# A plain second matrix product for the first 256-token unit, and its weight combinations spread out, in a fused attention and feed-forward kernel

## The chip, the core and the metric

The kernel runs on one core of one Trainium2 chip. The metric is the device time of one execution in microseconds (us); the profile is one more execution, recorded by the hardware profiler. The engines are TensorE (PE, with its weight loads as PEld), VectorE (DVE), ScalarE (ACT), GpSimd (POOL) and SyncE (SP, which issues nearly all the DMAs). Each engine works through its own instructions strictly in the order in which they were written, and they wait for each other by semaphores.

## What is computed

Attention in which each query keeps its 32 highest scores, for 8 batches of 8 heads with 576 tokens and 64 numbers per head, and then a two-layer feed-forward block on 4608 tokens:

```python
scores = q @ k.T / 8                   # per head, 576 x 576
kth    = the 32nd largest of each row
attn   = softmax(where(scores >= kth, scores, -1e9))
x      = (attn @ v), heads side by side # 4608 x 512
h      = x @ w_in                       # 512 -> 2048
g      = h - tanh(h)
out    = g @ w_out                      # 2048 -> 512
```

All in float32 on the chip.

## The kernel before, in words

**Steps.** The attention is cut into 144 steps; `plan` (L987) lists them. A step is one tile of 128 queries for a pair of heads. Batch 0 is steps 0 to 17, batch 1 is steps 18 to 35. The main loop (L1169) runs iteration n and works on several steps at once:

- `scores(n+1)` (L339): TensorE makes the scores of the next step in PSUM (L351), ScalarE copies them to SBUF (L359).
- `search(n)` (L362): VectorE finds the 32nd largest by folding (L381 to L389) and by rounds of MAX8 and MATCH_REPLACE8 (L393 to L404). It starts with L381, so the starts of L381 are the starts of the steps.
- `threshold(n)` (L409): GpSimd turns the result into a threshold, `tb` (L418), `nb` (L427).
- `mask(n-1)` (L430): ScalarE (L437) and GpSimd (L440, the tile `z`) strike out what is below the threshold; GpSimd notes a check in `bad` (L444).
- `expo(n-1)` (L456): ScalarE takes the exponentials (L460), GpSimd adds a small number to the sums in `rd` (L470).
- `invert(n-2)` (VectorE, L479, early in the search of iteration n), `divide(n-2)` (ScalarE, L486), `turn_z` (VectorE transposes the tile, L518, at the end of the search). `spread_keys` sends it through DRAM (L531, L534), and `values` (L568) multiplies by v on TensorE (L582). Batch 0 goes another way: TensorE transposes the tile.

**Units.** Tokens whose heads are all done form a unit: 256 tokens, except that the first 256 tokens of batch 0 are two units of 128. The feed-forward of a unit is a list of items (`ffn`, L965), appended to `work`, and `deal` (L1161) puts items between the attention's instructions, about three to a step. `rate` (L1143) sets how many: it spreads what is in `work` evenly until the next unit comes, using each unit's `items` (30 for 256 tokens).

**First matrix.** Items 0 to 15 of a 256-token unit (`ffn_full`, L956, which calls `ffn_h`, L630) are the product with `w_in`. `by_columns` (L623) splits each matmul into two halves of 64 output rows. After each odd item ScalarE takes tanh (L652) and a copy (L653), and GpSimd subtracts (L654, a 128x512 tensor).

**Second matrix.** For a 128-token unit it is plain: `ffn_o` (L656) adds 16 matmuls of 128x512 into one PSUM bank, ScalarE copies the bank (L671), SP sends it out (L673). For a 256-token unit it is Strassen-Winograd: seven products (`ORDER`, L830) of half-sized blocks in place of eight, as 14 items (`ffn_p`, L865; `product`, L836) of matmuls with 256 columns. The left factors need four sums of parts of g (`sum_up`, L817, GpSimd, L828: 8 tensors of 128x512 a unit, some issued as halves), the results need joins (L877, GpSimd).

**Weight combinations.** The right factors need T1 to T4, made once from `w_out` by `combine` (L690) on GpSimd: 16 subtractions of 128x512 (`COMBINE`, L709). `w_out` is four tensors of blocks b11, b12, b21, b22. T3 = b12 - b22 goes to the tensor `more`. T1 = b12 - b11 is written over b12 (L698), after which the plain second matrix can't be used any more. T2 = b22 - T1 (L700) and T4 = b21 - T2 (L705) follow; two halves of T2 and two of T4 are also stored in DRAM (`outgoing`, `send_kept`, L934; L702, L707), because `more` has room for only one of the two at a time: `bring` (L831, DMA L834) loads them back in items 4 and 11 of every unit's second matrix. `combine_next` (L939) does one combination per call, T3 from iteration 17 on, T2 and T4 from iteration 20 on; it is called by the second 128-token unit's `ffn_small_o` (L950) and by **every** item of `ffn_full`. In the profile the four T3 and the first T1 fall into the last items of the 128-token unit (214 to 226 us), and the other three T1, the four T2 and the four T4 into the first twelve items of the first 256-token unit (231 to 268 us).

Of the kernel before, what the change touches and what calls it, by code (L numbers as in the profile page):

```python
# [9 lines left out]
ALU = mybir.AluOpType  # L10
# [15 lines left out]
class Step:  # L26
# [4 lines left out]
    def __init__(self, b, hp, qt, unit, col, i=0, nq=1, pe=False, part=0):  # L31
        self.b, self.hp, self.qt, self.unit, self.col = b, hp, qt, unit, col
        self.part = 0 if pe else part
        self.i, self.nq, self.pe = i, nq, pe
        self.rem = qt == J
        self.last = i == nq - 1

        self.lag = 2 if pe else LAG


class Unit:
# [3 lines left out]
    def __init__(self, blocks, tag):  # L45
        self.blocks, self.tag = blocks, tag
        self.n = 128 * len(blocks)
        self.combines = False
        self.tail = False
        self.items = 16 if self.n == 128 else 30  # L50
        self.xT = None
        self.g = []
# [3 lines left out]
def kernel(  # L56
# [9 lines left out]
    nc = tc.nc  # L66
    P = nc.NUM_PARTITIONS
# [9 lines left out]
    CD = DM // P  # L77
    CF = DFF // P
# [4 lines left out]
    WJ = 4  # L83
# [32 lines left out]
    def next_h(name):  # L116
        bank[0] ^= 1
        return h_bank(bank[0], name)
# [19 lines left out]
    whole = {  # L138
        "T3": [more[:, 1024 * i : 1024 * (i + 1)] for i in range(2)],
        "T4": [more[:, 2048:3072], more[:, 3072:4096]],  # L140
        "T2": [more[:, 3072:4096], et_pe[:, 0:1024]],
    }
    whole = {x: [y.rearrange("p (m n) -> p m n", n=2 * P) for y in ys] for x, ys in whole.items()}
# [73 lines left out]
    def half(t):  # L217
        return slice(t * D, (t + 1) * D)
# [349 lines left out]
    def values(n):  # L568
# [41 lines left out]
        if n in done:  # L610
            work.extend(ffn(u))
# [44 lines left out]
    def ffn_o(u, i, part):  # L656
        if part == 0:
            cur[u] = next_h("ops")
        for f in range(2 * part, 2 * part + 2):
            o = f * u.n + i * P  # L660
            nc.tensor.matmul(
                cur[u][:],
                u.g[0][:, o // 512, o % 512 : o % 512 + P],
                w_out[f // FJ][:, f % FJ, :],
                start=(f == 0),
                stop=(f == CF - 1),
            )
        if part < CF // 2 - 1:
            return
        ot = thpool.tile([P, DM], FP32, tag="th", name="ot")  # L670
        nc.scalar.copy(ot[:], cur[u][:])  # L671
        for rows, dst in u.blocks[i]:
            nc.sync.dma_start(dst, ot[rows, :])  # L673
# [3 lines left out]
    def corners(x):  # L677
        x = x.rearrange("p (m r) n -> p m r n", r=2)
        return [[x[:, :, r, c * 2 * P : (c + 1) * 2 * P] for c in range(2)] for r in range(2)]
# [10 lines left out]
    def combine(x, j):  # L690

        (b11, b12), (b21, b22) = corners(w_out[j][:])
        k, ms = j // 2, slice(2 * (j % 2), 2 * (j % 2) + 2)
        t2 = whole["T2"][k][:, ms, :]
        if x == "T3":
            nc.gpsimd.tensor_tensor(whole["T3"][k][:, ms, :], b12, b22, ALU.subtract)
        elif x == "T1":
            nc.gpsimd.tensor_tensor(b12, b12, b11, ALU.subtract)  # L698
        elif x == "T2":
            nc.gpsimd.tensor_tensor(t2, b22, b12, ALU.subtract)  # L700
            if k == 0:
                outgoing.append((called[0], lambda: nc.sync.dma_start(kept["T2"][:, ms, :], t2)))  # L702
        else:
            t4 = temps[j % 2] if k else whole["T4"][k][:, ms, :]
            nc.gpsimd.tensor_tensor(t4, b21, t2, ALU.subtract)  # L705
            if k:
                outgoing.append((called[0], lambda: nc.sync.dma_start(kept["T4"][:, ms, :], t4)))  # L707

    COMBINE = [("T3", j) for j in range(WJ)] + [("T1", j) for j in range(WJ)]  # L709
    COMBINE += [(x, j) for j in (2, 3, 0, 1) for x in ("T2", "T4")]  # L710

    def quarters(u, k):

# [103 lines left out]
    def sum_up(u, k, x, ms=slice(0, 4)):  # L817

        (a11, a12), (a21, a22) = quarters(u, k)
        s1 = sums[k]  # L820
        out_, a, b, op = {
            "S1": (s1, a21, a22, ALU.add),
            "S3": (a21, a21, a11, ALU.subtract),
            "S2": (a11, s1, a11, ALU.subtract),
            "S4": (a12, a12, a11, ALU.subtract),
        }[x]
        engine = nc.vector if u.tail else nc.gpsimd
        engine.tensor_tensor(out_[:, ms], a[:, ms], b[:, ms], op)  # L828
# [102 lines left out]
    combined, now = [0], [0]  # L931
    called, outgoing = [0], []

    def send_kept(age):  # L934

        while outgoing and outgoing[0][0] <= called[0] - age:
            outgoing.pop(0)[1]()

    def combine_next():  # L939

        called[0] += 1
        send_kept(4)
        if combined[0] < len(COMBINE):
            x, j = COMBINE[combined[0]]
            if now[0] < (17 if x == "T3" else 20 if x in ("T2", "T4") else 0):
                return
            combine(x, j)
            combined[0] += 1

    def ffn_small_o(u, part):  # L950

        ffn_o(u, 0, part)
        if u.combines:
            combine_next()

    def ffn_full(u, item):  # L956

        ffn_h(u, item)
        combine_next()
        if item in (8, 9):  # L960
            sum_up(u, 0, ("S1", "S3")[item - 8])
        if item in (12, 13):
            sum_up(u, 1, ("S1", "S3")[item - 12], slice(0, 2))

    def ffn(u):  # L965

        nh = CF * u.n // (2 * P)
        full = len(u.blocks) == 2
        if u.tail:
            nh = 0  # L970
            for item in range(2 * len(ORDER)):
                yield CD * WJ, u, lambda item=item: ffn_s(u, item)
        for item in range(nh):
            f = (item + 1) * CF // nh - 1
            yield CD * (f // FJ + 1), u, lambda item=item: (ffn_full if full else ffn_h)(u, item)
        if not full:
            for part in range(CF // 2):
                yield CD * (WJ + part // 2 + 1), None, lambda part=part: ffn_small_o(u, part)
            return
        for item in range(2 * len(ORDER)):  # L980
            yield 2 * WJ * CD, None, lambda item=item: ffn_p(u, item)
# [5 lines left out]
    def plan():  # L987
        steps.clear(), done.clear()

        def block(b, qt):  # L990
            return [(slice(0, P), out[b * S + qt * P : b * S + (qt + 1) * P, :])]

        rest = None
        for b in range(B):
            if b % 4 == 0:
                rest = Unit(
                    [
                        [(half(i), out[(b + k + i) * S + JP : (b + k + i + 1) * S, :]) for i in range(2)]
                        for k in (0, 2)
                    ],  # L1000
                    "xTr",
                )

            parts = [(0, 1), (2, 3)]
            if b == 0:
                parts[0:1] = [(0,), (1,)]
            for a, qts in enumerate(parts):
                unit = Unit([block(b, qt) for qt in qts], "xT")
                unit.tail = b == B - 1 and a == len(parts) - 1
                if unit.tail:  # L1010
                    rest.tail = True
                    unit.items = rest.items = 4 * len(ORDER)
                pe = b == 0
                unit.combines = pe and a == 1
                for hp in range(NHP):
                    for i, qt in enumerate(qts):
                        steps.append(Step(b, hp, qt, unit, 0, i, len(qts), pe, a))
                    if hp == NHP - 1:
                        done[len(steps) - 1] = unit
                    if hp % 2 and a == (0 if b == B - 1 else len(parts) - 1):  # L1020
                        steps.append(Step(b, hp - 1, J, rest, b % 4 * R, pe=pe, part=a))
                        if hp == NHP - 1 and b % 4 == 3:
                            done[len(steps) - 1] = rest
        for g, after in zip(steps, steps[1:]):
            if after.pe and not after.rem and not g.pe:
                g.lag = 3
# [3 lines left out]

    def run(exact):
        plan()
        turned_pe[0] = not exact
        combined[0] = 0
# [237 lines left out]
```

## Time and profile before

| what | us |
|---|---|
| median of 3 timed runs (lowest, highest) | 1476.77 (1475.81, 1477.08) |
| time of the profiled execution | 1476.01 |
| its span, first to last instruction | 1474.2 |
| PE busy | 1365.6 (93%) |
| DVE busy | 1321.5 (90%) |
| POOL busy | 1090.2 (74%) |
| ACT busy | 1033.2 (70%) |
| start of step 20, 25, 50 (L381) | 227.88, 278.47, 490.81 |
| one 128x512 subtraction on POOL (L654) | 1.28 |
| one 128x576 subtraction on POOL (L440) | 1.44 |

How to read it: each row of a group names line, engine, operation, output and inputs; the busy time is the sum over the group. A timeline row gives start and duration, and in brackets how long the engine had stood idle and which instruction let it go on. A row of a windows table gives, for one stretch of time, how long each engine was busy in it; with the starts of L381 as borders each row is one step of the attention.

### The profile page before, as it was taken

How to read it: one execution, taken by the hardware profiler on the slowest of the kernel's cores; microseconds unless marked ns; L12 is line 12 of the kernel's file. 1: busy time of each engine (PE TensorE's matmuls, PEld its weight loads, DVE VectorE, ACT ScalarE, POOL GpSimd, SP SyncE). 2: the span in 40 equal slices, each digit the busy share in tenths (PEclk: the TensorE clock that was granted, in tenths of full speed). 3: DMA queues.
4: the chain of work that ended last, by engine and by line, in shares of the span. 5: the costliest groups of instructions: out<-in, count | busy, mean ns of one | idle time of the engine just before them, and what ended most of it. 6: DMA issues, size and time to landing. Idle time of an engine off the chain costs nothing.

```text
span 1474.2 us, 37773 instructions
## 1 busy us (share of the span) xinstructions
PE 1365.6 (93%) x13316; PEld 871.1 (59%) x13316; DVE 1321.5 (90%) x4968; ACT 1033.2 (70%) x1921; POOL 1090.2 (74%) x1581
## 2 busy tenths in 40 slices
PE   4667899889999898999999999999999999999998
PEld 2455565455565555656556666666565666656885
DVE  7999988899999999999999999999999999886411
ACT  4776677778787777777687777777777777664421
POOL 3777679968788686969696969696969697868211
PEclk9787999999999999999999999999999999999999
DMA  9955103676767676686767767777676667643320
GB/s 273 381 184 168 53 21 90 169 195 167 196 173 197 164 183 180 160 209 152 190 152 192 179 174 177 194 168 185 167 184 172 171 167 200 157 141 108 89 53 32
DMA packets 241255, 241.90 MB, mean 164 GB/s; under 512 B 177440, under 2 KB 186144, under 8 KB 233888
## 3 DMA queue, kind: packets, MB, share of 16 engines
q1 hardware_dynamic: 238688, 239.09, 60.7%
q8 instruction: 108, 1.77, 0.5%
q14 instruction: 91, 0.75, 0.2%
q10 hardware_dynamic: 2368, 0.30, 0.2%
HBM read 153.47 MB, written 85.85 MB: 162 GB/s over the span
## 4 chain that ended last, share of the span: by engine, by line
PE 46%; DVE 36%; POOL 9%; DMA 3%; ACT 3%; issue 2%; SPq 0%; DVEq 0%; ACTq 0%; POOLq 0%
PE hps L626 14%; PE hx L626 10%; PE hy L626 8%; DVE m L401 7%; PE av L582 5%; PE scps L351 5%; DVE top L393 5%; DVE rest L404 5%; DVE zx L518 5%; DVE ab L387 3%; POOL z L440 3%; DVE top L404 2%; DVE ab L382 2%; POOL g L654 2%; DVE scps L381 2%
## 5 line engine op out<-in xcount | busy, mean ns | idle before, releaser
L440 POOL TENSOR_TENSOR z<-sc,z 128x576 f32<-128x576 f32 x288 | 406.8, 1435 | 66.4 <-ACT z L437 66.0
L626 PE MATMUL hps<-xT,w_in 128*64 128x256 f32 x3584 | 412.2, 385 | 3.7 <-ACT g L653 3.7
L626 PEld LDWEIGHTS hps<-xT,w_in 128*64 128x64 f32 x3584 | 252.5, 138 | 157.1 <-issue 30.6
L486 ACT ACTIVATE z<-z,rd 128x576 f32<-128x576 f32 x252 | 181.2, 767 | 88.3 <-DVE rd L479 87.9
L460 ACT ACTIVATE z<-z,nb 128x576 f32<-128x576 f32 x288 | 221.9, 776 | 13.1 <-POOL z L440 13.0
L437 ACT ACTIVATE z<-sc,tb 128x576 f32<-128x576 f32 x288 | 208.3, 776 | 24.6 <-POOL tb L418 19.8
L654 POOL TENSOR_TENSOR g<-g,th 128x512 f32<-128x512 f32 x128 | 163.9, 1281 | 63.4 <-ACT g L653 61.9
L393 DVE MAX8 top<-ab 128x8 f32<-128x144 f32 x864 | 194.7, 296 | 0.0
L359 ACT COPY sc<-scps 128x1152 f32<-128x1152 f32 x144 | 161.0, 1118 | 44.7 <-PE scps L351 43.9
L351 PE MATMUL scps<-kT,qT 64*64 64x288 f32 x2016 | 154.6, 422 | 30.3 <-DVE top L389 27.1
L518 DVE STREAM_TRANSPOSE zx<-z 128x1152 f32<-128x1152 f32 x126 | 171.7, 1363 | 7.6 <-ACT z L486 5.1
L401 DVE MAX8 m<-rest 128x8 f32<-128x168 f32 x576 | 161.8, 323 | 0.0
L401 DVE MAX8 m<-top 128x8 f32<-128x144 f32 (+1 forms) x576 | 153.1, 308 | 0.0
L626 PE MATMUL hx<-w_out,g 128*64 128x256 f32 x1088 | 129.2, 385 | 2.5 <-POOL g L654 2.4
L626 PE MATMUL hy<-more,g 128*64 128x256 f32 x1088 | 125.4, 380 | 0.0
L351 PEld LDWEIGHTS scps<-kT,qT 64*64 64x64 f32 x2016 | 66.7, 133 | 97.6 <-issue 26.4
L418 POOL TENSOR_SCALAR tb<-m 128x1 f32<-128x1 f32 x288 | 85.9, 307 | 35.0 <-DVE m L401 34.6
L387 DVE TENSOR_TENSOR ab<-scps,sc 128x576 f32<-128x576 f32 x144 | 107.7, 748 | 0.0
L626 PEld LDWEIGHTS hx<-w_out,g 128*64 128x64 f32 x1088 | 76.2, 138 | 49.9 <-POOL g L654 5.7
L626 PEld LDWEIGHTS hy<-more,g 128*64 128x64 f32 x1088 | 76.7, 137 | 43.7 <-issue 6.7
L652 ACT ACTIVATE th<-hps 128x512 f32<-128x512 f32 x128 | 75.1, 587 | 38.7 <-PE hps L626 35.3
L444 POOL TENSOR_SCALAR bad<-top,tb 128x3 uint8<-128x3 f32 x288 | 96.6, 343 | 0.1
(215 smaller groups left out, 2464.7 us busy)
## 6 DMA issues: line engine op xcount, KB each, us to landing
there<-zx SPq DMA_DIRECT2D x56, 1152.0 KB, 4.8
spare<-there SPq DMA_DIRECT2D x224, 288.0 KB, 5.5
more<-kept_T SPq DMA_DIRECT2D x33, 512.0 KB, 4.2
there<-zx SPq DMA_DIRECT2D x14, 576.0 KB, 7.2
spare<-there SPq DMA_DIRECT2D x56, 144.0 KB, 3.2
out_dram<-ot SPq DMA_DIRECT2D x31, 256.0 KB, 3.0
vb<-in_v_dram SPq DMA_DIRECT2D x48, 128.0 KB, 5.0
kin<-in_k_dram SPq DMA_DIRECT2D x82, 72.0 KB, 4.4
```

Of the source, the lines that this page charges most:

```text
L351: nc.tensor.matmul(ps[i * R : i * R + w, t, s, 0:S2], qT[g.b, hp, g.part][half(t), o : o + w], kT[g.b, hp][half(t), ks], start=True, stop= ...
L359: nc.scalar.copy(sc[:], ps[:, :, :, 0:S2])
L387: nc.vector.tensor_tensor(low[:, :, :, 0:W2], thirds(near), thirds(far), ALU.min)
L393: nc.vector.max(top[:, t, o : o + 8], low[:, t, i, :])
L401: nc.vector.max(m[:, t, m8], seen[i][t])
L437: nc.scalar.activation(zv[:, t, :], scf[:, t, :], AF.Relu, bias=tb[:, t : t + 1], scale=-BIG)
L440: nc.gpsimd.tensor_tensor(zv[:, t, :], scf[:, t, :], zv[:, t, :], ALU.subtract)
L460: nc.scalar.activation(x["zv"][:, t, :], x["zv"][:, t, :], AF.Exp, bias=x["nb"][:, t : t + 1], scale=scale, accum_out=den[:, t : t + 1],)
L486: nc.scalar.activation(x, x, AF.Copy, scale=rds[n][:, g.i, t : t + 1])
L518: nc.vector.transpose(tiles(zx, g.nq)[:, :, :, g.i, :].rearrange("p c k j -> p k c j"), z[:].rearrange("p (k c j) -> p k c j", c=NG, j=G),)
L626: nc.tensor.matmul(acc[half(t)], lhs[:, half(t)], rhs, start=start, stop=stop, skip_group_check=True)
L654: nc.gpsimd.tensor_tensor(g, g, th[:], ALU.subtract)
```

## The change

The unit of the tokens 256 to 511 of batch 0, the first of 256 tokens, is marked `plain`. Its second matrix is no longer `ffn_p` but 16 items of `ffn_plain_o`: for each of its two blocks of 128 tokens eight calls of `ffn_o`, each with two of the 16 k-blocks, now through `by_columns` with 512 columns. Its `items` are 32 in place of 30. T1 is made last of all, and only in the items of the next unit, since it overwrites b12. T2 is computed as b11 - T3, which equals the old b22 - T1. `combine_next` is called on odd items only, in `ffn_full` and in `ffn_plain_o`, and `send_kept` waits two calls in place of four. The four sums of g, the joins and the two `bring` transfers of this one unit are not issued. All later units are as before.

In the order of the built instructions VectorE's list is identical before and after. On the other engines the lists differ from step 19 to about step 35, by single places in a few steps of the unit after that, and nowhere later.

```diff
+        self.plain = False
...
-            nc.tensor.matmul(
+            (by_columns if u.plain else nc.tensor.matmul)(
                 cur[u][:],
-                u.g[0][:, o // 512, o % 512 : o % 512 + P],
+                u.g[o // 2048][:, o % 2048 // 512, o % 512 : o % 512 + P],
                 w_out[f // FJ][:, f % FJ, :],
...
-            nc.gpsimd.tensor_tensor(t2, b22, b12, ALU.subtract)
+            nc.gpsimd.tensor_tensor(t2, b11, whole["T3"][k][:, ms, :], ALU.subtract)
...
-    COMBINE = [("T3", j) for j in range(WJ)] + [("T1", j) for j in range(WJ)]
-    COMBINE += [(x, j) for j in (2, 3, 0, 1) for x in ("T2", "T4")]
+    COMBINE = [("T3", j) for j in range(WJ)]
+    COMBINE += [(x, j) for j in (2, 3, 0, 1) for x in ("T2", "T4")] + [("T1", j) for j in range(WJ)]
...
-    def combine_next():
+    def combine_next(plain=True):
         called[0] += 1
-        send_kept(4)
+        send_kept(2)
         if combined[0] < len(COMBINE):
             x, j = COMBINE[combined[0]]
-            if now[0] < (17 if x == "T3" else 20 if x in ("T2", "T4") else 0):
+            if plain and x == "T1" or now[0] < (17 if x == "T3" else 20 if x in ("T2", "T4") else 0):
                 return
...
+    def ffn_plain_o(u, item):
+        ffn_o(u, item // (CF // 2), item % (CF // 2))
+        if item % 2:
+            combine_next()
+
     def ffn_full(u, item):
         ffn_h(u, item)
-        combine_next()
+        if item % 2:
+            combine_next(u.plain)
+        if u.plain:
+            return
...
+        if u.plain:
+            for item in range(CF):
+                yield 2 * WJ * CD, None, lambda item=item: ffn_plain_o(u, item)
+            return
...
+                unit.plain = pe and a == len(parts) - 1
+                if unit.plain:
+                    unit.items = 32
```

## The prediction, as put on record

> **What bounds the kernel now.** I took the starts of L381 first: in batch 1 a step takes 8.44 to 8.57 us as long as nothing holds VectorE up, and from step 25 to step 50 nearly all do. Just ahead of that, where the edited code runs, steps are longer. The table of windows with one row per step (20 to 25) shows it; its columns after the length are PE, PEld, DVE, ACT and POOL busy, the granted clock, the DMA share and GB/s.
>
> ```profile
> core 0: us, PE busy (x) PEld busy (x) DVE busy (x) ACT busy (x) POOL busy (x), PEclk, DMA share, GB/s
> 227.88:237.58 9.70, 9.70 (x123) 6.50 (x121) 8.51 (x33) 8.58 (x17) 9.54 (x15) 1.00 0.15 33
> 237.58:248.66 11.08, 10.33 (x94) 5.52 (x88) 8.66 (x34) 7.62 (x15) 10.91 (x16) 1.00 0.06 14
> 248.66:257.10 8.44, 5.97 (x44) 3.10 (x46) 8.40 (x34) 5.66 (x11) 8.28 (x11) 0.80 0.93 259
> 257.10:267.58 10.48, 9.71 (x96) 5.99 (x94) 8.60 (x35) 7.67 (x14) 10.32 (x13) 1.00 0.59 139
> 267.58:278.47 10.89, 8.50 (x66) 4.40 (x62) 8.72 (x36) 7.87 (x15) 10.72 (x16) 0.84 0.95 255
> 278.47:286.91 8.44, 6.13 (x64) 3.86 (x64) 8.40 (x35) 7.19 (x15) 8.19 (x16) 1.00 0.19 38
> ```
>
> In steps 21, 23 and 24 VectorE works only 8.6 to 8.7 us of 10.5 to 11.1, while POOL is busy nearly throughout; step 20 is another case, there PE is busy for all 9.70 us. The waits of VectorE from 237 to 279 us, and then those of POOL from 214 to 302 us:
>
> ```profile
> DVE rd L479 <- POOL rd L470: 4.8, 3, 2.4
> DVE top L389 <- POOL bad L444: 1.5, 1, 1.5
> DVE scps L381 <- ACT sc L359: 1.2, 1, 1.2
> ```
>
> ```profile
> POOL z L440 <- ACT z L437: 0.4, 1, 0.4
> ```
>
> So VectorE waits for POOL, and POOL for hardly anything: 85.7 us busy of those 88. Its timeline in step 23, and VectorE's wait that follows from it:
>
> ```profile
> 258.99 1.28 POOL L705 TENSOR_TENSOR more<-w_out,more 128x512 f32<-128x512 f32 x1
> 260.22 1.27 POOL L828 TENSOR_TENSOR et<-g 128x512 f32<-128x512 f32 x1
> 261.47 0.59 POOL L418 TENSOR_SCALAR tb<-m 128x1 f32<-128x1 f32 x2
> ...
> 262.36 0.23 POOL L470 TENSOR_SCALAR rd<-den 128x2 f32<-128x2 f32 x1
> 262.67 1.28 POOL L654 TENSOR_TENSOR g<-g,th 128x512 f32<-128x512 f32 x1
> ```
>
> ```profile
> 262.62 0.17 DVE L479 RECIPROCAL rd<-rd 128x2 f32<-128x2 f32 x1 [1.83 <-POOL rd L470]
> ```
>
> A combination (L705) and a sum of g (L828) stand ahead of the threshold and `rd` that VectorE needs.
>
> **What the Trainium skill says.** "GPSIMD Engine Reference", section 3.1, puts a two-input elementwise operation at about 2.6 cycles an element and 4497 ns for 2048 float32; a quarter, 1.1 us, is my estimate for 512. The trace has 1.24 to 1.28 us a tensor start to start, and I use 1.25. "TensorEngine Tiling (Array Packing)", section Key Properties, says that tiles work in parallel. The trace agrees at 256 columns: an item of halves (16 records) takes as long as the same work at full width (two k-blocks of 128x512, 4 records), 1.76 to 1.8 us:
>
> ```profile
> 199.97 3.60 PE L661 MATMUL ops<-w_out,g 128*128 128x512 f32 x8
> ```
>
> ```profile
> 256.14 3.67 PE L626 MATMUL hps<-xT,w_in 128*64 128x256 f32 x32
> ```
>
> No run here shows halves with 512 columns. "TensorE: Matmul & The Clock Gate", section What's actually happening, says an idle window halves the array's clock. The trace agrees in part: after 2.62 us without work scores took 1.62 us in place of 1.20 (at 251.12) and the windows above show 0.80 and 0.84; after 3.45 us (at 314.81) they took 1.20 all the same.
>
> **The change part by part.** A batch-1 step costs POOL 2.78 (L440 twice) + 0.60 (bad) + 1.17 (tb, nb, rd) = 4.55 us. In 8.5 us that leaves room for (8.5 - 4.55)/1.25 = 3.2 tensors of 512.
>
> *Combinations and sums around steps 20 to 24.* I counted the other POOL tensors between the `z` pairs of consecutive steps, z(18) to z(24), by the order of the built instructions. Before: 3 (and two small xTr), 4, 5, 6, 1.6, 2.6 (a half counts 0.6); the z pairs of the trace are 9.10, 9.52, 10.73, 12.03, 6.49 and 7.76 us apart, and 4.55 + 1.25 x 6 = 12.05 confirms the price. After: 1 (and xTr), 4, 2, 2, 4, 2, and then 1. So the three intervals of 9.5 to 12.0 us become 9.55, 7.05 and 7.05, and the overload is gone.
>
> *Does the step then reach VectorE's own time?* `rd` is needed 3.45 us after the start of a step (237.58 to 241.03, where L479 began to wait), and the threshold ahead of it may begin 7.1 us after the start of the step before, 1.34 us ahead. With 1.17 us for tb, nb and rd, POOL may be 1.34 + 3.45 - 1.17 = 3.6 us late. I walked the new order through steps 21 to 25 with durations of the trace. The threshold begins at 238.9, 247.3, 256.9, 264.2, 273.7; `rd` is ready 1.0, 1.1, -0.1, 1.1 and 0.1 us ahead of its need. So some 0.1 us of waiting stays, and two steps have no reserve. ScalarE's copy of the next scores is ready 0.8, 0.5, 0.6 and 1.2 us early.
>
> *Gain.* Steps 21 to 24 took 11.08 + 8.44 + 10.48 + 10.89 = 40.89 us, and VectorE was busy for 8.66 + 8.40 + 8.60 + 8.72 = 34.38. The difference is 6.5 us. Less 0.1 for the wait and 0.2 for the thin reserves: **-6.2 us**. The 1.2 us of step 20 stay, being PE's (no idle from 218.9 on), and PE's list is the same up to there.
>
> *PE.* The unit's second matrix goes from 14 items at 1.76 = 24.6 to 16 at 1.76 = 28.2: +3.5 us. Hidden: a step with three items is 3 x 1.76 + 1.13 (scores) + 1.1 (half of a `values` of 2.16) + 0.4 (transposes) = 7.9 us of 8.5, and in steps 25 to 30, where the plain items lie, PE waits today for VectorE's L389 (2.31, 1.33 and 3.45 us). Without that cover it costs the 3.5. The order has three items in each step from 21 to 29, and the next unit begins no later against the steps. For a 512-column item I take the full-width price, 1.76; the lower end is the same, since the same columns stream; the upper, if the halves took turns, is 3.5.
>
> *T1, moved into the next unit.* Around steps 30 to 35 POOL's counts become 4, 2, 5, 3.2, 3.2, 3.6, over the room at times; walked through in the same way, it is up to 2.5 us late, within the 3.6 that cost nothing: 0. T1 waits for the plain items' reads of w_out, which PE finished a step earlier; queued behind it are the threshold and `rd` of that step, and behind those VectorE. If the reserve is gone, each tensor costs VectorE up to 1.25.
>
> *ScalarE.* Seven copies of 0.36 us become two of 0.59: -1.3 us, off the path.
>
> *DMAs and SP's queue.* Two loads of 512 KB are not issued (7.4 us to landing, beside other transfers), two stores of 256 KB out go earlier. On SP the stores of kept T2 wait for their POOL subtraction at 264.2 and 273.7; ahead of them stand the transfer of the transposed tile and the loads, which end near 267 and 272, and behind the second stands a tile transfer that waits for L518 to about 280. So nothing waits: 0. The first `values` of batch 1 needs its tile at 259.8, and I have it landed at about 258.5: 1.3 us of reserve.
>
> *Sum.* Later instruction lists are nearly the same and VectorE's is identical, so the 6.2 us go through to the end. The profiled execution was 1476.01 us (its span of 1474.2 and 1.8 around it), 0.76 below the median; both move alike: 1476.01 - 6.2 = 1469.8, against the median 1476.77 - 6.2 = 1470.6.
>
> **The rivals.** *Halves take turns at 512 columns.* A 512-float output fills its PSUM bank, and only 256 columns have been seen to overlap. A step has room for (8.5 - 1.13 - 1.1 - 0.3)/3 = 2.0 us an item, so the loss is 16 x (item - 2.0) against a gain of 6.2: slower than before from 2.4 us an item, and at 3.5 it is 24 - 6 = +18, 1495 us. Against it: the 256-column rows. *The queue moves.* T1 beside sums and g's in steps 30 to 33 exceeds the reserve, or the two tight steps miss it; some 3 us come back: 1473.6. For it, reserves of 0 to 1.1 us; against it, only isolated tensors are left. *PE takes over.* With POOL gone PE fills 7.9 of 8.5 us; a late tile or a clock of 0.8 in two steps costs 2 x 1.2: 1473. *The change doesn't do what it says*, because the shift is taken up by PE's waits after step 50 (steps of 8.8 to 10 us there): 1476.8. Against it, those follow the same lists. *More*: step 20's 1.2 and some later waits go too: 1468.
>
> **How the numbers follow.** Forecast 0.62, more 0.07, queue moves or PE takes over 0.14, no effect 0.11, halves in turn 0.06. "Faster by over 0.2%" means over 2.95 us, about what a measurement tells from no change: 0.62 + 0.07 + 0.11 of the 0.14 = 0.80. Within: 0.03 + 0.11 = 0.14. Slower: 0.06. The range reaches from 1467.0 (a gain of 9.8, all of step 20 and 2.4 later) to 1474.2 (the partial cases with 0.6 for the median's own spread); it leaves out no effect and halves in turn.
>
> **What would show it.** Right: L381 of step 25 at about 272 in place of 278.47, step 50 at about 484.6, VectorE's waits for POOL in steps 21 to 24 under 0.5 us, no `sum_up` before step 32, plain items of 8 records in 1.76 us. Wrong: L479 waiting for `rd` in steps 22, 24 or 30 to 35, plain items over 2 us, or the lead of step 50 lost before the end.

## The result and the profile after

| | kernel before | changed kernel |
|---|---|---|
| median of the first timed runs, us | 1475.7 (6 runs, 1473.45 to 1477.08) | 1468.05 (6 runs, 1466.62 to 1470.23) |
| ratio to before, 95% interval | | 0.9951, 0.9938 to 0.9964 |
| time of the profiled execution, its span | 1476.01, 1474.2 | 1468.51, 1466.6 |
| POOL busy, PE busy | 1090.2, 1365.6 | 1078.7, 1366.4 |
| start of step 20, 25, 50 | 227.88, 278.47, 490.81 | 226.03, 270.08, 482.39 |
| steps 20 to 24 together | 50.59 | 44.05 |
| steps 25 to 30 together | 50.88 | 50.87 |

The changed kernel is faster by 7.65 us, and the place is the one that the prediction named: five steps lost 6.54 us, the six after them nothing. From here on line numbers of the changed kernel are one higher than those of before in this region (L381 is L382, L470 is L471, L479 is L480). "Steps 20 to 24" always means the time from the start of step 20 to the start of step 25.

The table of windows of the changed kernel, one row for each of the steps 20 to 25, with the columns that the table of before has:

```profile
226.03:235.74 9.71, 9.71 (x123) 6.51 (x121) 8.52 (x34) 8.59 (x17) 9.46 (x16) 1.00 0.15 33
235.74:244.33 8.59, 8.59 (x82) 4.90 (x78) 8.56 (x34) 7.04 (x13) 6.87 (x10) 1.00 0.08 18
244.33:252.77 8.44, 8.44 (x83) 4.96 (x80) 8.40 (x35) 7.94 (x17) 8.14 (x13) 1.00 0.90 260
252.77:261.51 8.74, 8.06 (x82) 5.01 (x80) 8.50 (x34) 6.88 (x15) 8.56 (x13) 1.00 0.63 136
261.51:270.08 8.57, 8.52 (x64) 3.62 (x62) 8.54 (x36) 7.91 (x16) 8.41 (x12) 1.00 0.92 263
270.08:278.52 8.44, 6.83 (x54) 2.90 (x52) 8.40 (x35) 6.14 (x13) 8.26 (x14) 1.00 0.63 132
```

In steps 21 to 24 (rows two to five) the length is now VectorE's own busy time to within 0.24 us. POOL dropped from 10.91 to 6.87 us in step 21. Step 20 is as long as before, with PE busy throughout. The granted clock is 1.00 in every row, where it had 0.80 and 0.84 in two steps.

The waits of VectorE from 235 to 271 us, of the changed kernel (in all, times, longest):

```profile
DVE scps L382 <- ACT sc L360: 1.2, 1, 1.2
DVE rd L480 <- POOL rd L471: 0.2, 1, 0.2
```

The 4.8 us for `rd` are 0.2, and the 1.5 for `bad` are gone. The 1.2 for ScalarE's copy of the scores belong to step 20. POOL's timeline in step 23, and VectorE's `rd` there:

```profile
252.92 1.28 POOL L655 TENSOR_TENSOR g<-g,th 128x512 f32<-128x512 f32 x1
254.16 1.27 POOL L706 TENSOR_TENSOR spare<-w_out,et 128x512 f32<-128x512 f32 x1
255.42 0.58 POOL L419 TENSOR_SCALAR tb<-m 128x1 f32<-128x1 f32 x2
255.96 0.25 POOL L428 TENSOR_SCALAR nb<-m 128x2 f32<-128x2 f32 x1
256.30 0.23 POOL L471 TENSOR_SCALAR rd<-den 128x2 f32<-128x2 f32 x1
```

```profile
256.56 0.17 DVE L480 RECIPROCAL rd<-rd 128x2 f32<-128x2 f32 x1 [0.20 <-POOL rd L471]
```

Two tensors stand ahead of the threshold, as before: now the subtraction for g (L655) and a combination, then a combination and a sum of g. What has changed is when POOL comes to them: 0.15 us after the start of the step (252.92 against 252.77) in place of 1.89 us (258.99 against 257.10). Between the two `z` pairs ahead of them it has two tensors to make where it had five. The wait is 0.20 in place of 1.83 us. It is the step that the walk had given a reserve of -0.1 us.

### The profile page after: what moved, and what is told of

It reads as the page before. It is cut to its first block, busy times and chain, and to the rows that moved or that the text cites. A ratio compares the mean times of both kernels' runs of the same rounds, so it can differ in the third digit from the quotient of the medians.

```text
span 1466.6 us, 37560 instructions
## 1 busy us (share of the span) xinstructions
PE 1366.4 (93%) x13220; PEld 864.3 (59%) x13220; DVE 1321.3 (90%) x4968; ACT 1032.7 (70%) x1916; POOL 1078.7 (74%) x1568
## 4 chain that ended last, share of the span: by engine, by line
PE 43%; DVE 37%; POOL 7%; DMA 5%; ACT 4%; issue 2%; SPq 1%; ACTq 0%; DVEq 0%; POOLq 0%
PE hps L627 13%; PE hx L627 10%; PE hy L627 8%; DVE m L402 7%; PE av L583 5%; PE scps L352 5%; DVE top L394 5%; DVE zx L519 5%; DVE rest L405 5%; DVE ab L388 3%; POOL z L441 2%; DVE top L405 2%; DVE ab L383 2%; DMA there<-zx 2%; DVE scps L382 2%
## 5 line engine op out<-in xcount | busy, mean ns | idle before, releaser
L655 POOL TENSOR_TENSOR g<-g,th 128x512 f32<-128x512 f32 x128 | 164.2, 1283 | 63.1 <-ACT g L654 61.5
L627 PE MATMUL hx<-w_out,g 128*64 128x256 f32 x1024 | 123.3, 390 | 2.5 <-POOL g L655 2.4
L419 POOL TENSOR_SCALAR tb<-m 128x1 f32<-128x1 f32 x288 | 86.4, 310 | 45.4 <-DVE m L402 44.9
L627 PE MATMUL hy<-more,g 128*64 128x256 f32 x1024 | 117.8, 380 | 0.0
L627 PEld LDWEIGHTS hx<-w_out,g 128*64 128x64 f32 x1024 | 72.4, 139 | 47.7 <-POOL g L655 5.6
L627 PEld LDWEIGHTS hy<-more,g 128*64 128x64 f32 x1024 | 72.3, 137 | 40.8 <-issue 5.4
```

The lines of the kernel that those rows point to most:

```text
L627: nc.tensor.matmul(acc[half(t)], lhs[:, half(t)], rhs, start=start, stop=stop, skip_group_check=True)
L655: nc.gpsimd.tensor_tensor(g, g, th[:], ALU.subtract)
```

## The experiments

Each is an edit of the changed kernel. Times of stretches are taken between starts of L382 in the profiled execution, because they are free of what happens elsewhere. Some of the expectations name a stretch by the step at whose start it ends: their "steps 25 to 32" are steps 25 to 31 here. In the changed kernel steps 20 to 24 took 44.05, 20 to 25 52.49, 25 to 30 50.87 and 30 to 35 51.01 us.

| run | steps 20 to 24, us | steps 25 to 30, us | median, us | ratio to before, 95% |
|---|---|---|---|---|
| e1_dense | 46.36 | 50.89 | 1471.53 | 0.9962 (0.9947 to 0.9976) |
| e2_spread_only | 44.08 | 58.74 | 1480.01 | 1.0018 (1.0000 to 1.0035) |
| e3_sums_back | 46.48 | 51.88 | 1472.46 | 0.9974 (0.9964 to 0.9984) |
| e4_plain_twice | 44.04 | 70.44 | 1489.57 | 1.0081 (1.0053 to 1.0109) |
| e5_t1_twice | 44.03 | 50.88 | 1473.84 | 0.9980 (0.9970 to 0.9989) |
| e6_full_width | 44.03 | 50.89 | 1470.36 | 0.9962 (0.9948 to 0.9977) |
| e7_spread_early_t1 | 46.93 | 52.52 | 1475.22 | 0.9988 (0.9980 to 0.9996) |
| e8_later_items | 42.46 | 51.44 | 1465.73 | 0.9917 (0.9899 to 0.9935) |
| e9_changed_again | 44.03 | 50.86 | 1469.11 | 0.9949 (0.9931 to 0.9967) |
| e9_later_again | 42.47 | 51.39 | 1465.57 | 0.9925 (0.9904 to 0.9946) |

**Combinations in every item again.** The plain matrix stays, the spreading over odd items goes for this unit.

```diff
-        if item % 2:
+        if item % 2 or u.plain:
             combine_next(u.plain)
```

> The changed kernel with one part undone: the combinations are made on every item of the plain unit again, not on every second (T1 still in the next unit). POOL's tensors between the z pairs z(18) to z(24) become 1, 5, 3, 4, 2, 1 in place of 1, 4, 2, 2, 4, 2. Theory (a tensor costs VectorE time only where POOL comes over 3.6 us late with rd): walked through from the changed kernel's trace, rd comes 0.4 us late in step 22 and 2.5 us late in step 23, so steps 20 to 24 together take 47.0 us (44.05 changed, 50.59 before) and the time is about 2.9 us above the changed kernel's. Rival (the plain second matrix alone brings the gain, and the spreading brings nothing): 44.1 us.

Steps 20 to 24 took 46.36 us, 2.3 more than in the changed kernel; step 23 took 10.76. VectorE's `rd` in that step:

```profile
260.90 0.17 DVE L480 RECIPROCAL rd<-rd 128x2 f32<-128x2 f32 x1 [2.22 <-POOL rd L471]
```

The wait comes back with the dense list and no other edit, so the spreading is worth about 2.3 us with the plain matrix in place. The granted clock is 1.00 in steps 22 and 23 of this run, so such a wait does not need the 0.80 and 0.84 that the kernel before had.

**Spreading without the plain matrix.** The unit has its Strassen second matrix again; combinations come in odd items of both matrices, and T1 still comes last.

```diff
     def ffn_p(u, item, finish):
+        if item % 2:
+            combine_next(False)
...
-            combine_next(u.plain)
-        if u.plain:
-            return
+            combine_next()
...
-                unit.plain = pe and a == len(parts) - 1
-                if unit.plain:
-                    unit.items = 32
```

> The other part alone: the first 256-token unit keeps the seven products with their sums and joins; the combinations are made on every second item of its first matrix, T2 as b11 - T3, and T1 in four of the items of its second matrix. POOL's counts from z(18) to z(27) become 1, 2, 4, 4, 2.6, 4.6, 4.2, 4.6, 1, 1.6. Theory: the room of 3.2 tensors a step is exceeded from step 23 on, by some 6 us added up at step 26, of which 3.6 are free; steps 20 to 29 take about 88.5 us (86.5 changed, 93.0 before), so the spreading alone brings about two thirds of the gain, and the rest of it comes late, in steps 25 to 27. Rival (the plain product is what counts): about 93. Second rival (spreading is all): 86.5.

Steps 20 to 29 took 94.38 us, far from the expected 88.5. Steps 20 to 24 reached 44.08, the changed kernel's time; but steps 27 and 28 took 11.33 and 13.38 us. The waits of that stretch, from 288 to 322 us of this kernel:

```profile
PEld hx L627 <- POOL w_out L699: 9.7, 3, 4.0
PE hx L627 <- POOL w_out L699: 8.4, 3, 3.5
ACT ot L923 <- PE hx L627: 4.9, 1, 4.9
DVE scps L382 <- ACT sc L360: 4.9, 1, 4.9
```

TensorE waits for T1 (L699), which this unit's own products need, and the scores queue up behind those products, and VectorE behind the scores. The expectation had counted what POOL does to `rd` but no deadline for T1. So the run shows two things: spreading, with T1 out of the way, ends the backlog of steps 20 to 24 without the plain matrix, and T1 can't be put last while its own unit needs it.

**Spreading, T1 in time.** Again without the plain matrix, but with T1 made where it was before, in every item; only T2 and T4 are spread.

```diff
-    COMBINE = [("T3", j) for j in range(WJ)]
-    COMBINE += [(x, j) for j in (2, 3, 0, 1) for x in ("T2", "T4")] + [("T1", j) for j in range(WJ)]
+    COMBINE = [("T3", j) for j in range(WJ)] + [("T1", j) for j in range(WJ)]
+    COMBINE += [(x, j) for j in (2, 3, 0, 1) for x in ("T2", "T4")]
...
     def ffn_p(u, item, finish):
+        if item < 2:
+            combine_next()
...
-        if item % 2:
-            combine_next(u.plain)
-        if u.plain:
-            return
+        if item % 2 or combined[0] < 2 * WJ:
+            combine_next()
```

> Spreading alone again, without the plain product, with T1 where the kernel before had it (the last item of the small unit and the first three of this one), T2 as b11 - T3 and T2, T4 on every second item from then on. POOL's counts from z(18) to z(25): 3, 3, 4, 4, 2.6, 4.6, 4.2, 2.6. The run before, with T1 in the items of the second matrix, waited for T1 on TensorE (10 us); here T1 is early, so that wait is gone. Theory: the lateness adds up to about 4 us at most, so about 1 us is paid; steps 20 to 30 take about 87.5 us (86.5 changed, 93.0 before). Rival (without the plain product the sums and combinations can't fit, whatever their order): 90 or more.

Steps 20 to 29 took 91.01 us against 93.03 before and 86.48 in the changed kernel. The rival holds: T1 is still dense in step 21 (11.10 us), and steps 24, 26 and 27 are over their floor. VectorE's waits from 226 to 320 us of this kernel:

```profile
DVE rd L480 <- POOL rd L471: 4.4, 4, 2.4
```

Spreading T2 and T4 alone is worth 2.0 of the 6.5 us (1.6 by step 50). The other 4.5 come with the plain product, and the waits that are left say what of it counts, the work that it takes from POOL: the wait of 2.4 us stands behind the dense T1, and the other three, 2.0 us together, fall where POOL also makes the sums of g (L829) and, in step 27, a join (L880).

**The sums put back.** The plain matrix stays, and POOL makes two of the four sums of g (four tensors) that nobody reads, in items 8, 9, 12 and 13 of the unit's first matrix, where the later units make theirs.

```diff
         if u.plain:
+            if item in (8, 9, 12, 13):
...
+                nc.gpsimd.tensor_tensor(sums[k][:, ms], a21[:, ms], b[:, ms], op)
             return
```

> The changed kernel with four POOL tensors put back: in items 8, 9, 12 and 13 of the plain unit the sums S1 and S3 that the seven products would need are computed (two of 512, two of 256 numbers a partition) into a scratch place that nothing reads. PE, ScalarE and the DMAs have no work more. Theory: rd comes 2.9 us late in step 23 in place of 0.2, and 1.2 us late in step 25; steps 20 to 25 take 56.1 us in place of 52.5. Rival (POOL's load doesn't matter, the gain came from PE, whose products no longer wait for sums, or from the two loads of 512 KB that are gone): 52.5.

Steps 20 to 25 took 55.92 us. POOL's timeline of this kernel ahead of the late threshold in step 23, and VectorE's wait:

```profile
253.48 1.29 POOL L974 TENSOR_TENSOR et<-g 128x512 f32<-128x512 f32 x1
254.73 1.27 POOL L655 TENSOR_TENSOR g<-g,th 128x512 f32<-128x512 f32 x1
255.95 1.28 POOL L706 TENSOR_TENSOR spare<-w_out,et 128x512 f32<-128x512 f32 x1
257.18 1.28 POOL L974 TENSOR_TENSOR et<-g 128x512 f32<-128x512 f32 x1
```

```profile
259.58 0.17 DVE L480 RECIPROCAL rd<-rd 128x2 f32<-128x2 f32 x1 [2.65 <-POOL rd L471]
```

Two of the extra sums (L974) make the wait of 2.65 us in the step without reserve. The sums belong to no engine but POOL, and PE's list and the DMAs are those of the changed kernel, so it is POOL's order that decides, as the prediction had it.

**Full width.** The plain items with whole matmuls.

```diff
-            (by_columns if u.plain else nc.tensor.matmul)(
+            nc.tensor.matmul(
```

> The changed kernel with the plain items as full-width matmuls of 128x512 in place of halves of 64 rows. Theory (halves overlap at 512 columns as they do at 256): the same time within 0.5 us in steps 25 to 30, items of 1.76 us in both. Rival (halves take turns in part): steps 25 to 30 shorter here than in the changed kernel.

Steps 25 to 30 took 50.89 against 50.87 us. Two plain items of the changed kernel as halves, and then of this one at full width:

```profile
284.79 3.65 PE L627 MATMUL ops<-w_out,g 128*64 128x512 f32 x16
```

```profile
286.70 3.60 PE L662 MATMUL ops<-w_out,g 128*128 128x512 f32 x8
```

3.65 for 16 records in halves, 3.60 for 8 at full width, and the first records of the two halves start 0.01 us apart: the halves run beside each other at 512 columns as well. That agrees with the Trainium skill, "TensorEngine Tiling (Array Packing)", section Key Properties, on tiles that work in parallel; the 512-column case, which the prediction could not see, is hereby measured.

**Each plain matmul twice.** This gives the rival's price, twice 1.8 us an item. The copy out is scaled by 0.5, so every product is counted twice and halved.

```diff
+            for again in range(2 if u.plain else 1):
                 (by_columns if u.plain else nc.tensor.matmul)(
...
-                start=(f == 0),
-                stop=(f == CF - 1),
+                    start=(f == 0 and again == 0),
+                    stop=(f == CF - 1 and again == (1 if u.plain else 0)),
```

> The changed kernel with every matmul of the plain second matrix issued twice into the same sums, and the sums halved when they are copied out: an item of 3.5 us in place of 1.76, which is the price that the first rival gave to halves that take turns. Theory of the prediction: a step has room for 2.0 us an item, so the loss is 16 x 1.5 = 24 us against the changed kernel, about 16 slower than before; TensorE starts with a reserve of some 3.7 us (its scores at step 26 wait for VectorE), so steps 25 to 32 take 80 to 83 us in place of 59.4. Rival (TensorE catches up later, in steps 31 to 50): the loss at step 50 is clearly less than at step 32.

Steps 25 to 31 took 79.04 in place of 59.43 us, +19.6, just under the expected 80 to 83, and nothing of it came back: from step 20 to step 50 it is 276.74 against 256.36, +20.4. Steps 25 and 26 of this kernel, the first at its floor, the second not, and the wait of VectorE that ends the second:

```profile
272.51:280.95 8.44, 8.44 (x52) 2.78 (x50) 8.41 (x34) 4.39 (x9) 8.26 (x14) 1.00 0.62 131
280.95:294.67 13.72, 13.72 (x86) 5.31 (x84) 8.73 (x35) 5.66 (x11) 4.63 (x9) 1.00 0.75 195
```

```profile
294.68 0.47 DVE L382 TENSOR_TENSOR scps<-scps,sc 128x288 f32<-128x288 f32 x1 [4.57 <-ACT sc L360]
```

PE is busy for 100% of both rows. Only in the second does VectorE wait (8.73 busy of 13.72), for scores that stand behind the items. The median is 13.9 us above that of before, where the rival had +18: its mechanism is real at that price, and its premise is what failed.

**T1 twice.** After each T1 POOL makes it once more into a tensor that is free then.

```diff
+            x1 = sums[1].rearrange("p m n -> p (m n)").rearrange("p (m n) -> p m n", m=2)
+            nc.gpsimd.tensor_tensor(x1, b12, b11, ALU.subtract)
```

> The changed kernel with each of the four T1 in the next unit followed by a second POOL subtraction of the same size into a scratch place that nothing reads, so that POOL's counts around steps 30 to 33 go from 4, 2, 5, 3.2 to 6, 3, 6, 3.2. Theory (3.6 us of lateness are free, what is beyond is paid in full): rd comes 2.7 us late in step 33 and 0.9 in step 34, so steps 30 to 36 take 54.6 us in place of 51.0. Rival (POOL's lateness is always hidden there): 51.0. Second rival (each tensor is paid): 56.0.

Steps 30 to 35 took 55.15 us, 4.1 more than the changed kernel; steps 33 and 34 took 11.72 and 9.41. POOL's timeline of this kernel in step 33, and the wait that follows:

```profile
340.96 1.28 POOL L655 TENSOR_TENSOR g<-g,th 128x512 f32<-128x512 f32 x1
342.20 1.28 POOL L699 TENSOR_TENSOR w_out<-w_out 128x512 f32<-128x512 f32 x1
343.55 1.27 POOL L701 TENSOR_TENSOR et<-w_out 128x512 f32<-128x512 f32 x1
344.82 0.58 POOL L419 TENSOR_SCALAR tb<-m 128x1 f32<-128x1 f32 x2
```

```profile
345.95 0.17 DVE L480 RECIPROCAL rd<-rd 128x2 f32<-128x2 f32 x1 [3.06 <-POOL rd L471]
```

Four extra tensors are 5.0 us of POOL's time, and 4.1 of it reach VectorE. So T1 lies just inside what POOL can be late with in the changed kernel: once it costs nothing, twice nearly everything.

**Fewer items ahead of step 20.** Step 20's 1.2 us had been left to PE. Iterations 11 to 20 deal out four fifths of their share, so that 20 items and not 23 stand between the scores of step 12 and those of step 21.

```diff
+            if 11 <= n <= 20:
+                share *= 0.8
```

> The changed kernel with the planner's share cut to 0.8 in iterations 11 to 20, so that TensorE gets 20 items in place of 23 between the scores of steps 12 and 21, and the three come in steps 23 to 30, where TensorE has had to wait for VectorE. Theory (steps 12 to 20 are bound by TensorE, by the instruction count that the planner gave them): steps 12 to 21 take about 5 us less than the 75.5 of the changed kernel, and steps 21 to 31 keep their 85.2, since the reserve of TensorE there is 3.7 us. Rival (the three items are paid in full later): the sum of both stays at 160.7.

Steps 12 to 20 took 72.64 us against 75.51 in the changed kernel's profile, steps 13 to 20 64.34 against 67.80; steps 21 to 30 took 85.44 against 85.21. The gain is there, 2.9 to 3.5 us where 5 were expected.

**Both once more, on one chip.** The changed kernel unedited, and the version with later items.

> The changed kernel once more, with nothing edited. Theory: of the 7.6 us by which its first runs lay below the kernel before, 6.5 are the change's (steps 21 to 24) and 1.1 is scatter of stretches whose instruction lists are the same in both, above all the start-up. Then steps 20 to 24 take 44.0 to 44.1 us again, step 14 starts anywhere between 175 and 179.3 us, and the median over the median before, run in turn on the same chip, is 0.9951 to 0.9960. Rival: the change also shortens something ahead of step 14 or after step 50. Then step 14 starts near 175.1 again, steps 50 to 74 take 223.4 again, and the ratio is 0.9945 to 0.9950.

> The version with the items between steps 12 and 20 put later, once more and now on the same chip as the changed kernel. Theory: it is 3.0 to 3.5 us faster than the changed kernel in steps 12 to 30, and so is the median (near 1465). Rival: the lead found on another chip was scatter of the start-up; then the stretch of steps 12 to 30 repeats, and the median is within 1.5 us of the changed kernel's.

The changed kernel's stretch repeats: 44.03 us. Its step 14 started at 177.22 us, against 175.14 in its first profile and 176.99 before, and steps 50 to 74 took 221.78, against 223.38 and 222.17. So neither of those two differences is the change's. The ratio, 0.9949, lies where the rival had it, but its interval covers both. The version with later items took 158.07 us from step 12 to step 30 against 161.60, which is 3.5 less, and its median is 3.5 us lower. Its interval overlaps that of the changed kernel, so the medians alone don't settle it; the stretch does. Step 12 varies by itself (see the last section), but from step 13 to step 30 the version took 149.79 and 149.72 us in its two profiles and the changed kernel 153.01 and 152.96: 3.2 us less. Steps 14 and 20 of the changed kernel in its second profile, then of the version with later items:

```profile
177.22:186.77 9.55, 9.55 (x82) 7.82 (x81) 7.21 (x34) 6.72 (x14) 6.73 (x12) 1.00 0.06 15
228.10:237.81 9.71, 9.71 (x123) 6.50 (x121) 8.52 (x34) 8.59 (x17) 9.45 (x16) 1.00 0.15 33
```

```profile
174.33:181.52 7.19, 7.19 (x63) 5.92 (x58) 7.16 (x33) 5.66 (x11) 5.43 (x11) 1.00 0.09 21
223.00:231.48 8.48, 8.48 (x98) 4.88 (x96) 8.44 (x34) 7.27 (x14) 6.93 (x14) 1.00 0.26 68
```

Step 14 falls from 9.55 to 7.19 us and step 20 from 9.71 to 8.48, both to VectorE's busy time; VectorE's waits for scores from step 12 to step 20 fall from 9.4 to 5.7 us. Some of it is given back in steps 15 (7.27 to 8.13) and 25 (8.44 to 8.97).

## Why the prediction was right, step by step

- **Bound and place.** VectorE waited for POOL's `rd` in steps 21, 23 and 24, and those are the steps that became shorter: 11.08, 8.44, 10.48 and 10.89 us are 8.59, 8.44, 8.74 and 8.57. Undoing a part of it on POOL alone brought waits back (combinations dense again +2.3 us, two sums +3.4 in steps 20 to 25), with the work of the other engines left alone.
- **The walk along POOL's list.** The changed profile's stretch begins 1.85 us earlier (226.03 against 227.88). With that added, the thresholds (L419) at 237.09, 245.72, 255.42, 262.52 and 272.06 us are 238.94, 247.57, 257.27, 264.37 and 273.91, where the prediction had 238.9, 247.3, 256.9, 264.2 and 273.7: at most 0.4 us apart. The one wait is 0.20 us, predicted 0.1. One reading was slightly off: where nothing holds it up, `rd` (L479) starts 3.50 us into a step, not 3.45.
- **The size.** Steps 21 to 24 lost 40.89 - 34.34 = 6.55 us, predicted 6.2. The mis-sized term is VectorE's busy time: the same instructions show 34.00 us busy in place of 34.38. The idle time left, 0.34 us, is what the prediction allowed, 0.3. The records suggest why the busy sum fell: the durations of the single records fell only from 43.05 to 42.95 us in sum, far above the busy time because neighbouring records overlap, and a wait between two of them undoes an overlap. Step 22 shows 8.50 us busy with a wait of 0.19 in e1_dense and 8.40 without one here. So length less busy time counts each wait some 0.1 us too small, and the kernel before had four in these steps. No run tested this by itself.
- **Step 20 stays.** 9.71 against 9.70, PE busy throughout. That it can be had was shown by dealing items later.
- **PE.** The 3.5 us of the larger second matrix are hidden: steps 25 to 30 took 50.87 against 50.88. The room of 2.0 us an item agrees with e4_plain_twice: an item takes 3.5 us there, 16 x (3.5 - 2.0) is 24 us, and 20.4 were lost. The 3.6 between them are about the reserve that PE brings along, put at 3.7 in that run's expectation; the first rival's +18 had left it out. The 7.9 of 8.5 us that PE fills by the prediction's prices can't be read off a busy share: steps 21 and 22 show PE busy for 8.59 of 8.59 and 8.44 of 8.44 us, and VectorE waits for nothing in them.
- **T1.** Cost 0, as predicted: steps 30 to 35 took 51.01 against 51.02. The 3.6 us that POOL may be late are borne out within about 0.5 us: worked out with them, T1 doubled was to cost 3.6, and it cost 4.1.
- **Halves at 512 columns.** 3.65 us for two items against 3.60 at full width. The lower end of the price was the right one.
- **DMAs and SP.** VectorE and PE's matmuls show no wait for a transfer in steps 20 to 24; PE's weight loads show one of 0.8 us in step 24, where the matmuls are busy for 8.52 of 8.57 us. The first `values` began at 258.14 (259.99 with the shift; predicted 259.8), with no idle time ahead of it.
- **The whole run.** The forecast was 1470.6 us and the first median 1468.05: 1.1 of these 2.5 us lie in the median of before, which was 1475.7 in this comparison and 1476.77 when the forecast was made. The medians moved by 7.65 and, in the second comparison, by 7.1 us, more than the 6.55 of the mechanism. In the two profiles of the first comparison, which are 7.50 us apart, the parts are -1.85 ahead of step 20, -6.54 in steps 20 to 24, -0.03 up to step 50, +1.2 from step 50 to 75, and -0.3 after that and around the span. The first and the fourth did not repeat. What is left, 0.5 to 1.1 us, is smaller than the half-width of the interval (0.0013 x 1476 = 1.9 us), and the runs don't tell it from scatter.
- **The rivals.** "The queue moves" happens only with work added (T1 made twice, or the sums put back). "PE takes over" did not: the clock was 1.00 in all five steps. "No effect" did not: the lead from step 20 to step 50 is 6.57 us, and step 143 still starts 7.1 us earlier. "More" was wrong too: step 20 stayed, and that the median lies on its figure is the baseline and the scatter named above, not its mechanism.

What the change is made of, in steps 20 to 29: spreading T2 and T4 alone gave 2.0 us; the plain matrix without the spreading 4.2; both 6.5. With T1 put last but its unit not plain, the five steps reach their floor, and 7.9 us are lost afterwards.

## What to carry to other kernels

When an engine that is not the bound holds up the one that is, take the order of its instructions, add up how late each due result comes and compare it with how late it may come; here four tensors inside that reserve cost nothing, and four more cost 4.1 of their 5.0 us. Before work is moved later, look for everyone who reads its result: the 7.9 us that e2_spread_only lost came from a deadline on another engine, not from the queue. An engine that is busy for 100% of a step is the bound only if the next engine is seen to wait.

## What the runs showed that was not expected

- Stretches with the same instruction list take different times from run to run. Over ten profiled executions whose lists are the same up to there, step 14 starts anywhere from 175.14 to 179.26 us: step 7 took 15.50 to 16.73 us, step 9 15.58 to 16.73, step 12 7.62 to 8.73. Steps 50 to 74 took 221.78 to 223.38 us in the same ten. These are as large as effects that one wants to measure, which is why stretches were compared and not whole times. The granted clock goes with it. Step 7 of the second profile of the version with later items, whose lists are the same as far as step 10, and then of e2_spread_only:

```profile
92.34:106.49 14.15, 9.66 (x86) 8.41 (x86) 13.70 (x43) 9.90 (x21) 10.96 (x14) 0.99 0.70 242
93.22:109.94 16.72, 12.27 (x86) 10.86 (x86) 13.72 (x43) 10.02 (x21) 10.96 (x14) 0.80 0.60 206
```

In all twelve profiles step 7 took 14.15 us at a granted clock of 0.99 (once), 15.50 to 15.79 at 0.87 to 0.89, and 16.72 to 16.73 at 0.80; step 9 took under 15.8 at 0.89 and over 16.6 at 0.80. Why the clock differs from execution to execution stays open.

- In the version with later items PE still shows 100% busy in steps 14 and 20, though those are up to 2.4 us shorter and VectorE fills all but 0.04 us of them. A busy share of 100% alone does not tell whether PE sets the length of a step.
